# Leaky relu out of PSUM: one parametric relu on ScalarE in place of a multiplication there and a maximum on VectorE

## The chip, the core and the metric

The kernel runs on one core of a Trainium2 chip. The metric is the device time of one execution in microseconds. Before the change three runs gave a median of 1226.71 us (1224.39 to 1227.79). The engines are called as in the profile: PE is TensorE's matmul, PEld its weight load, DVE is VectorE, ACT is ScalarE, POOL is GpSimd, SP is the queue that issues the transfers.

## What is computed

Chunked attention, then two feed-forward layers on its 3072 tokens of 512 features, all in fp32:

```python
scores = scale * np.matmul(q_c, k_full.transpose(0, 1, 3, 2))
...
x = np.ascontiguousarray(attn_out.transpose(0, 2, 1, 3)).reshape(B * S, H * D)
h = x @ w_in                      # 512 -> 2048
g = np.maximum(0.01 * h, h)       # the leaky relu of this change
x = (g @ w_out)                   # 2048 -> 512
return (x @ w_a) * (x @ w_b) @ w_out2
```

## The kernel before

Every fp32 product is made of three matmuls on a high and a low part (`mm3`, L301): a float is cast to fp32r for the high part (an ACT cast), and the difference is the low part (a subtraction on DVE or POOL). So each operand of TensorE costs two passes ahead of it.

The attention works in 24 units of 128 tokens: scores on PE (L202), softmax on DVE and ACT (L215 to L233), turning the probabilities by sixteen 32x32-block transpositions on DVE (`a_turn`, L246; the first four units do it on PE), the product with v on PE (`a_pv`, L276), and hi and lo parts of the result (`a_out`, L289 on ACT, L290 on DVE).

The first feed-forward layer goes over six blocks of 512 tokens (`bi`), and in each over sixteen chunks of 128 hidden features (`f`). `mm1` (L377) makes 12 matmuls into a PSUM tile `h` (two buffers), then the leaky relu: ACT multiplies `h` by 0.01 into `t` (L383), DVE takes the maximum of `t` and `h` into `g` (L385). `split_g` (L317) makes the parts `gh` (ACT, L320) and `gl` (L321, on POOL in the first block, on DVE in the others). `mm2` (L388) adds the chunk's 12 matmuls into four accumulators `a`; it runs two chunks behind `mm1` (`LAG`). In the first block the chunks are halves of 256 tokens that run three chunks apart, so there are 19 steps instead of 16.

Beside the first block the weights are decoded: a raw pair of words is biased on ACT (L79), joined on DVE by three instructions (`w_join`, L83, L86, L87), cast on ACT (L93) and subtracted on POOL (L94) into `w`, which `mm1` and `mm2` of that chunk wait for. There are 32 of these. Beside blocks 1 to 4 the same is done for the second layer's weights (`prep_steps`, tiles `pz`, `ps`, `pw`), whose results go to DRAM. The units of the next block's attention run beside each block.

The second feed-forward layer (`layer3`, `layer4`, L668 on) has products on PE, copies on ACT and sums on DVE; the change does not touch it. Nothing sets the order by hand: the source gives the program's order, and a scheduler that is part of the framework places each engine's instructions from it. Each engine then runs its list in order, and an instruction that waits holds up what stands behind it.

Of the kernel before, what the change touches and what calls it, by code (L numbers as in the profile page):

```python
# [7 lines left out]
F32 = mybir.dt.float32  # L8
F32R = mybir.dt.float32r
I32 = mybir.dt.int32  # L10
AF = mybir.ActivationFunctionType
ALU = mybir.AluOpType
AX = mybir.AxisListType

P = 128
# [11 lines left out]
TB = 512  # L27
# [4 lines left out]
def kernel(  # L32
# [10 lines left out]
    nc = tc.nc  # L43
# [11 lines left out]
    tp = ctx.enter_context(tc.tile_pool(name="tp", bufs=4, side="right"))  # L55
# [251 lines left out]
    def proj(ps, slot, x, c):  # L307
        hi, lo = x
        for kc in range(KC):
            mm3(  # L310
                ps[:, c],
                (slot[:, 0, kc * P:kc * P + P], slot[:, 1, kc * P:kc * P + P]),
                (hi[:, kc, c], lo[:, kc, c]),
                kc == 0, kc == KC - 1,
            )

    def split_g(g, c, eng):  # L317
        gh = tp.tile([P, TB], F32R, tag="gh", name="gh", bufs=3)
        gl = tp.tile([P, TB], F32R, tag="gl", name="gl", bufs=3)
        nc.scalar.copy(gh[:, c], g[:, c])  # L320
        eng.tensor_tensor(  # L321
            out=gl[:, c], in0=g[:, c], in1=gh[:, c].bitcast(F32), op=ALU.subtract
        )
        return gh, gl
# [52 lines left out]
    def mm1(bi, parts):  # L377
        ps = ps_h.tile([P, TB], F32, tag="h", name="h")
        for o, n, f in parts:
            proj(ps, wslot[f, 0], x1["x", bi], slice(o, o + n))  # L380
        c = slice(min(o for o, _, _ in parts), max(o + n for o, n, _ in parts))
        t = tp.tile([P, TB], F32, tag="t", name="t")
        nc.scalar.mul(t[:, c], ps[:, c], 0.01)  # L383
        g = tp.tile([P, TB], F32, tag="t", name="g")
        nc.vector.tensor_tensor(out=g[:, c], in0=t[:, c], in1=ps[:, c], op=ALU.max)  # L385
        return split_g(g, c, nc.gpsimd if bi == 0 else nc.vector)

    def mm2(bi, parts, g):  # L388
# [201 lines left out]
    for n, (bi, f, parts) in enumerate(items):  # L590
# [10 lines left out]
        if first:  # L601
            W1.load(2 * f + 14)
            W1.step(nc.gpsimd)
        behind.append((bi, parts, mm1(bi, parts)))
        if first:
            W1.step(nc.gpsimd)
# [226 lines left out]
```

## Time and profile before

| | |
|---|---|
| median of three runs | 1226.71 us (1224.39 to 1227.79) |
| the profiled execution | 1226.21 us, its span 1224.4 us |
| PE, DVE, ACT, POOL busy | 96%, 61%, 31%, 12% of the span |
| mean granted clock of TensorE | 0.982 |
| first layer (with attention and weights) | about 20 to 590 us |
| second layer | about 590 us to the end |

A row of a group gives its count, the busy time, the mean of one instruction in ns, and the idle time of the engine just before it with what ended that. A row of a timeline gives start and duration in us, and in brackets the idle time before. The clock of a stretch is a share of full speed: 1.00 is 2.4 GHz, 0.5 is 1.2 GHz.

### The profile page before, as it was taken

What the parts mean: (1) busy time and instruction counts of PE and PEld (TensorE: products, weight loads), DVE (VectorE), ACT (ScalarE), POOL (GpSimd) and SP (SyncE); (2) the same over time, 40 slices, a digit from 0 to 9 for tenths busy, and PEclk for the clock granted to TensorE, in tenths of its full rate; (3) what the DMA queues carried; (4) which work ended last, traced back from release to release, by engine and by line L of the source; (5) the groups of instructions that cost most, each with busy time, mean ns of one, the idle gap of its engine ahead of it and who ended that gap; (6) DMA issues with size and microseconds to landing.
All of it is one profiled execution on the core that took longest, in us unless ns stands there. A gap on an engine that the chain in (4) does not pass through costs nothing.

```text
span 1224.4 us, 16825 instructions
## 1 busy us (share of the span) xinstructions
PE 1170.7 (96%) x6632; PEld 984.1 (80%) x6632; DVE 752.9 (61%) x1313; ACT 383.1 (31%) x642; POOL 145.4 (12%) x109
## 2 busy tenths in 40 slices
PE   5788799989998999999999999999999999999998
PEld 5778788867887887888888888888888888888887
DVE  5999959795897899666622443447443447433443
ACT  3634333243334433222422222224122223222220
POOL 1544512032122222000000000000000000000000
PEclk9898999989999999999999999999999999999999
DMA  9766658768887887642633843537453535453512
GB/s 322 256 229 194 210 186 306 268 238 299 297 304 254 310 311 261 212 138 86 221 106 108 319 158 120 193 125 280 162 215 130 198 131 208 158 204 120 189 61 103
DMA packets 63822, 250.72 MB, mean 205 GB/s; under 512 B 7424, under 2 KB 8832, under 8 KB 56832
## 3 DMA queue, kind: packets, MB, share of 16 engines
q1 hardware_dynamic: 63744, 249.66, 57.5%
q8 instruction: 52, 0.85, 0.3%
q14 instruction: 26, 0.21, 0.1%
HBM read 200.34 MB, written 49.28 MB: 204 GB/s over the span
## 4 chain that ended last, share of the span: by engine, by line
PE 67%; DVE 2%; DMA 1%; issue 0%; POOL 0%; SPq 0%; DVEq 0%; POOLq 0%
PE o L729 5%; PE o L730 5%; PE o L731 5%; PE A L662 4%; PE A L663 4%; PE A L664 4%; PE h L303 4%; PE a L403 4%; PE a L404 4%; PE a L400 4%; PE h L304 3%; PE h L305 3%; PE C L662 3%; PE C L663 3%; PE C L664 3%; PE D L663 1%
## 5 line engine op out<-in xcount | busy, mean ns | idle before, releaser
L303 PE MATMUL h<-xh,w 128*128 128x512 f32 (+1 forms) x448 | 168.8, 377 | 17.5 <-POOL w L94 14.7
L400 PE MATMUL a<-gh,w 128*128 128x512 f32 (+1 forms) x448 | 161.3, 360 | 4.8 <-DVE x L412 2.3
L304 PE MATMUL h<-xl,w 128*128 128x512 f32 (+1 forms) x448 | 164.2, 367 | 0.5 <-DVE xl L290 0.5
L305 PE MATMUL h<-xh,w 128*128 128x512 f32 (+1 forms) x448 | 163.7, 365 | 0.0
L403 PE MATMUL a<-gl,w 128*128 128x512 f32 (+1 forms) x448 | 160.8, 359 | 0.0
L404 PE MATMUL a<-gh,w 128*128 128x512 f32 (+1 forms) x448 | 160.8, 359 | 0.0
L303 PEld LDWEIGHTS h<-xh,w 128*128 128x128 f32 x448 | 87.5, 195 | 33.2 <-POOL w L94 15.7
L729 PE MATMUL o<-w,cl 128*128 128x512 f32 x288 | 112.1, 389 | 0.2 <-DMA w<-wod 0.2
L730 PE MATMUL o<-w,ch 128*128 128x512 f32 x288 | 112.0, 389 | 0.0
L731 PE MATMUL o<-w,ch 128*128 128x512 f32 x288 | 112.0, 389 | 0.0
L385 DVE TENSOR_TENSOR g<-t,h 128x512 f32<-128x512 f32 (+1 forms) x99 | 66.1, 668 | 67.3 <-ACT t L383 66.5
L320 ACT CAST gh<-g 128x512 fp32r<-128x512 f32 (+1 forms) x99 | 60.1, 607 | 149.5 <-DVE g L385 144.1
L246 DVE STREAM_TRANSPOSE pt<-p 32x128 f32<-32x128 f32 x320 | 96.8, 302 | 5.5
L400 PEld LDWEIGHTS a<-gh,w 128*128 128x128 f32 x448 | 84.6, 189 | 18.6 <-DVE x L412 2.9
L304 PEld LDWEIGHTS h<-xl,w 128*128 128x128 f32 x448 | 87.7, 196 | 13.1 <-DVE xl L290 0.9
L305 PEld LDWEIGHTS h<-xh,w 128*128 128x128 f32 x448 | 87.0, 194 | 13.3
L404 PEld LDWEIGHTS a<-gh,w 128*128 128x128 f32 x448 | 84.7, 189 | 12.5
L403 PEld LDWEIGHTS a<-gl,w 128*128 128x128 f32 x448 | 84.6, 189 | 12.5
L383 ACT ACTIVATE t<-h 128x512 f32<-128x512 f32 (+1 forms) x99 | 57.5, 581 | 110.3 <-PE h L305 110.3
L684 DVE TENSOR_TENSOR ga<-u,C 128x512 f32<-128x512 f32 x36 | 24.8, 688 | 105.4 <-ACT u L676 76.2
L676 ACT COPY u<-A 128x512 f32<-128x512 f32 x72 | 42.3, 587 | 143.5 <-PE A L664 143.5
L662 PE MATMUL A<-ch,wab 128*128 128x512 f32 x216 | 84.1, 389 | 0.0
(95 smaller groups left out, 2116.3 us busy)
## 6 DMA issues: line engine op xcount, KB each, us to landing
wab<-wab SPq DMA_DIRECT2D x36, 1792.0 KB, 7.3
w<-wod SPq DMA_DIRECT2D x116, 512.0 KB, 4.7
raw<-w SPq DMA_DIRECT2D x68, 512.0 KB, 5.9
wab<-pw SPq DMA_DIRECT2D x12, 1792.0 KB, 6.7
k<-kl SPq DMA_DIRECT2D x48, 256.0 KB, 4.3
v<-vl SPq DMA_DIRECT2D x48, 256.0 KB, 4.7
wod<-w SPq DMA_DIRECT2D x16, 512.0 KB, 5.3
q<-ql SPq DMA_DIRECT2D x48, 128.0 KB, 4.1
```

Of the source, the lines that this page charges most:

```text
L246: nc.vector.transpose(out=pt[o0:o0 + 32, :, 2 * cpar + hpar, hpx, :], in_=p[i0:i0 + 32, hpx::2, 32 * b:32 * b + 32],)
L303: nc.tensor.matmul(ps, w[1], x[0], start=first, stop=False)
L304: nc.tensor.matmul(ps, w[0], x[1], start=False, stop=False)
L305: nc.tensor.matmul(ps, w[0], x[0], start=False, stop=last)
L400: nc.tensor.matmul(ps, slot[:, 1, c], gh[:, t], start=f == 0 and o == 0, stop=False, **kw)
L403: nc.tensor.matmul(ps, slot[:, 0, c], gl[:, t], start=False, stop=False, **kw)
L404: nc.tensor.matmul(ps, slot[:, 0, c], gh[:, t], start=False, stop=f == NF1 - 1, **kw)
L662: nc.tensor.matmul(ps, w[:, 1, i, c], hi[:, kc], start=first and kc == 0, stop=False, **kw)
L663: nc.tensor.matmul(ps, w[:, 0, i, c], lo[:, kc], start=False, stop=False, **kw)
L729: nc.tensor.matmul(o, cl[:, q], w[:, 0, :], start=k == 0, stop=False)
L730: nc.tensor.matmul(o, ch[:, q], w[:, 1, :], start=False, stop=False)
L731: nc.tensor.matmul(o, ch[:, q], w[:, 0, :], start=False, stop=k == NCH - 1)
```

## The change

`mm1` no longer makes `t`. ACT reads `h` from PSUM and writes `g` at once, with a parametric relu whose slope below zero is 0.01.

```diff
         c = slice(min(o for o, _, _ in parts), max(o + n for o, n, _ in parts))
-        t = tp.tile([P, TB], F32, tag="t", name="t")
-        nc.scalar.mul(t[:, c], ps[:, c], 0.01)
         g = tp.tile([P, TB], F32, tag="t", name="g")
-        nc.vector.tensor_tensor(out=g[:, c], in0=t[:, c], in1=ps[:, c], op=ALU.max)
+        nc.scalar.activation(g[:, c], ps[:, c], AF.Prelu, alpha=0.01)
         return split_g(g, c, nc.gpsimd if bi == 0 else nc.vector)
```

99 maxima leave DVE; 99 ACT instructions become another function with the same operands. One tile of the four-buffer tag `t` is taken for each chunk instead of two. Lines behind 383 are two lower in the new kernel. The list of ACT still begins with one load of activation tables and holds no other. The lists of PE are alike but for six small products at the end of the first block, which stand ahead of two matmuls instead of behind them. The lists of DVE and ACT are re-placed by the scheduler at many places; three of them follow.

DVE in the first block, the sixteenfold transposition of the second unit that DVE turns (before; `pt` is the turned probabilities, `z` a joined weight):

```order
L233 TENSOR_TENSOR p<-p,l 128x512
L87 SCALAR_TENSOR_TENSOR z<-raw,z 128x512
L246 STREAM_TRANSPOSE pt_139<-p 32x4x32 x7
L385 TENSOR_TENSOR g<-t,h 128x512
L246 STREAM_TRANSPOSE pt_139<-p 32x4x32 x9
L86 SCALAR_TENSOR_TENSOR z<-raw,z 128x512
```

The same place now:

```order
L233 TENSOR_TENSOR p<-p,l 128x512
L83 TENSOR_SCALAR z<-raw 128x512
L246 STREAM_TRANSPOSE pt_139<-p 32x4x32 x16
L86 SCALAR_TENSOR_TENSOR z<-raw,z 128x512
L87 SCALAR_TENSOR_TENSOR z<-raw,z 128x512
```

The maximum has left the middle of the transpositions, which now stand in one piece.

DVE in the third block (`bi` = 2), the sixteenfold transposition of the last unit turned there (`ps` and `pz` belong to the second layer's weights), before:

```order
L493 TENSOR_TENSOR ps<-pz,ps 128x256
L246 STREAM_TRANSPOSE pt_139<-p 32x4x32 x6
L385 TENSOR_TENSOR g<-t,h 128x512
L246 STREAM_TRANSPOSE pt_139<-p 32x4x32 x4
L321 TENSOR_TENSOR gl<-g,gh 128x512
L246 STREAM_TRANSPOSE pt_139<-p 32x4x32 x6
L83 TENSOR_SCALAR pz<-raw 128x512
```

and now:

```order
L491 TENSOR_TENSOR ps<-pz,ps 128x256
L233 TENSOR_TENSOR p<-p,l 128x512
L246 STREAM_TRANSPOSE pt_139<-p 32x4x32 x16
L321 TENSOR_TENSOR gl<-g,gh 128x512 x2
L83 TENSOR_SCALAR pz<-raw 128x512
```

Here the subtraction `gl` has moved behind the sixteen transpositions too.

ACT in the first block, two chunks (`w<-z` is the cast of a joined weight), before:

```order
L383 ACTIVATE t<-h 128x512
L79 ACTIVATE raw<-raw 128x512
L93 CAST w<-z 128x512
L320 CAST gh<-g 128x512
L79 ACTIVATE raw<-raw 128x512
L93 CAST w<-z 128x512
L79 ACTIVATE raw<-raw 128x512
L383 ACTIVATE t<-h 128x512
```

and now:

```order
L383 ACTIVATE g<-h 128x512
L79 ACTIVATE raw<-raw 128x512
L320 CAST gh<-g 128x512
L79 ACTIVATE raw<-raw 128x512
L93 CAST w<-z 128x512 x2
L79 ACTIVATE raw<-raw 128x512
L93 CAST w<-z 128x512
L383 ACTIVATE g<-h 128x512
```

The cast `gh` stands closer behind the instruction that reads `h`, and what it waits for is now ACT's own work.

## Rows read from the trace of the kernel before

**Rows 1.** The page's busy time of each engine, its share of the span and its instructions.

```profile
PE 1170.7 (96%) x6632; PEld 984.1 (80%) x6632; DVE 752.9 (61%) x1313; ACT 383.1 (31%) x642; POOL 145.4 (12%) x109
```

**Rows 2.** The table of stretches: start and end, length, busy time of PE, PEld, DVE, ACT and POOL (with counts), granted clock, share of the DMA engines, GB/s.

```profile
28.00:152.00 124.00, 99.96 (x918) 95.81 (x919) 118.02 (x186) 57.27 (x101) 62.24 (x45) 0.89 0.68 225
152.00:180.00 28.00, 26.03 (x198) 24.14 (x197) 13.82 (x35) 8.34 (x19) 4.59 (x5) 0.94 0.57 201
...
236.00:274.00 38.00, 32.46 (x205) 26.17 (x204) 36.20 (x77) 14.13 (x25) 10.00 (x6) 0.91 0.69 255
...
320.00:384.00 64.00, 60.51 (x386) 49.88 (x385) 60.09 (x120) 24.22 (x41) 15.84 (x10) 0.97 0.78 279
384.00:590.00 206.00, 204.38 (x1300) 169.37 (x1299) 149.86 (x312) 69.30 (x116) 26.53 (x18) 1.00 0.65 224
590.00:1224.00 634.00, 630.71 (x2779) 520.93 (x2777) 283.91 (x406) 161.79 (x261) 0.00 (x0) 1.00 0.46 167
```

**Rows 3.** Who waited for whom over the whole execution: total us, times, longest.

```profile
ACT gh L320 <- DVE g L385: 144.1, 81, 6.8
...
ACT t L383 <- PE h L305: 110.3, 51, 3.9
...
PE pv L276 <- DVE pt L246: 18.5, 16, 2.7
...
PE h L303 <- POOL w L94: 14.7, 6, 5.8
...
PE a L400 <- DVE x L412: 2.3, 1, 2.3
```

**Rows 4.** The maxima on DVE in the stretch from 28 to 152 us, by shape.

```profile
L385 DVE TENSOR_TENSOR g<-t,h 128x512 f32<-128x512 f32 x12 | 8.1, 678 | 0.1
...
L385 DVE TENSOR_TENSOR g<-t,h 128x256 f32<-128x256 f32 x2 | 0.8, 412 | 0.0
```

**Rows 5.** Shortest, median and longest of the instructions that write or read `g` on DVE.

```profile
L385 DVE TENSOR_TENSOR g<-t,h x99: 402/686/691, 24.8 to 673.7; 128x512 f32<-128x512 f32 x93, 128x256 f32<-128x256 f32 x6
...
L321 DVE TENSOR_TENSOR gl<-g,gh x80: 636/692/1770, 175.6 to 675.1; 128x512 fp32r<-128x512 f32 x80
```

**Rows 6.** The same for the last instruction of a weight's join, whose two inputs are both in SBUF.

```profile
L87 DVE SCALAR_TENSOR_TENSOR z<-raw,z x32: 676/693/1786, 18.6 to 147.5; 128x512 int32<-128x512 int32 x32
```

**Rows 7.** DVE's timeline in the first block: the first and the last of the 14 maxima between 28 and 152 us, and between them two others, each of these with the instruction behind it.

```profile
40.55 0.42 DVE L385 TENSOR_TENSOR g<-t,h 128x256 f32<-128x256 f32 x1
...
57.78 0.68 DVE L385 TENSOR_TENSOR g<-t,h 128x512 f32<-128x512 f32 x1
58.38 1.46 DVE L87 SCALAR_TENSOR_TENSOR z<-raw,z 128x512 int32<-128x512 int32 x1
...
85.37 0.68 DVE L385 TENSOR_TENSOR g<-t,h 128x512 f32<-128x512 f32 x1
85.97 0.68 DVE L86 SCALAR_TENSOR_TENSOR z<-raw,z 128x512 int32<-128x512 int32 x1
...
149.08 0.67 DVE L385 TENSOR_TENSOR g<-t,h 128x512 f32<-128x512 f32 x1
```

**Rows 8.** DVE's timeline in the two later runs without slack: the first and the last of the four maxima of the first run and the `gl` behind the last; then, of the second run, the first and the last of three maxima, and the maximum and the `gl` that stand inside the transpositions from 370.9 to 378.5 us.

```profile
242.08 0.69 DVE L385 TENSOR_TENSOR g<-t,h 128x512 f32<-128x512 f32 x1
...
262.46 0.69 DVE L385 TENSOR_TENSOR g<-t,h 128x512 f32<-128x512 f32 x1
...
264.46 1.75 DVE L321 TENSOR_TENSOR gl<-g,gh 128x512 fp32r<-128x512 f32 x1
...
344.64 0.68 DVE L385 TENSOR_TENSOR g<-t,h 128x512 f32<-128x512 f32 x1
...
367.01 0.68 DVE L385 TENSOR_TENSOR g<-t,h 128x512 f32<-128x512 f32 x1
...
372.81 0.69 DVE L385 TENSOR_TENSOR g<-t,h 128x512 f32<-128x512 f32 x1
...
374.81 1.75 DVE L321 TENSOR_TENSOR gl<-g,gh 128x512 fp32r<-128x512 f32 x1
```

**Rows 9.** PE's timeline behind these two places: what waited, and the first-layer matmuls that follow.

```profile
267.52 0.47 PE L276 MATMUL pv<-pt,v 128*64 128x64 f32 x2 [2.71 <-DVE pt L246]
...
270.50 0.80 PE L303 MATMUL h<-xh,w 128*128 128x512 f32 x1
...
273.61 0.40 PE L304 MATMUL h<-xl,w 128*128 128x512 f32 x1
273.84 0.40 PE L305 MATMUL h<-xh,w 128*128 128x512 f32 x1
...
377.25 0.33 PE L276 MATMUL pv<-pt,v 128*64 128x64 f32 x2 [2.53 <-DVE pt L246]
...
379.57 0.80 PE L303 MATMUL h<-xh,w 128*128 128x512 f32 x1
...
382.73 0.42 PE L304 MATMUL h<-xl,w 128*128 128x512 f32 x1
```

**Rows 10.** ACT's instructions of this size by line: the multiplication that goes, and the exponential of the softmax.

```profile
L383 ACT ACTIVATE t<-h 128x512 f32<-128x512 f32 x93 | 55.2, 594 | 104.9 <-PE h L305 104.9
...
L220 ACT ACTIVATE p<-p 128x512 f32<-128x512 f32 x24 | 15.1, 631 | 47.0 <-DVE p L217 47.0
```

**Rows 11.** The multiplication in the stretch from 28 to 152 us.

```profile
L383 ACT ACTIVATE t<-h 128x512 f32<-128x512 f32 x12 | 7.1, 588 | 0.0
```

## The prediction

> **What bounds the kernel now.** I read the busy shares first. PE is busy 96% of the span, DVE 61%, ACT 31% [rows 1]. The average says that PE is the bound and that an engine at 61% hardly matters; the table of stretches says where that is false. From 590 us to the end PE is busy 630.7 of 634 us, and from 384 to 590 it is busy 204.4 of 206 [rows 2]. No cheaper relu shortens those. PE's gaps lie earlier: 24.0 us between 28 and 152, 2.0 up to 180, 5.5 between 236 and 274 and 3.5 between 320 and 384, each the length less PE's time. One more wait of 2.3 us is for a copy of an accumulator [rows 3]. In three of these stretches DVE is busy 118.0 of 124, 36.2 of 38 and 60.1 of 64 us [rows 2]. So there are places where DVE has no slack, and PE stands idle in just these.
>
> The list of waits tells what PE stands for there: 18.5 us for the product with v behind DVE's transpositions, 14.7 us for first-layer products behind POOL's subtraction of a weight [rows 3]. The second looks like POOL's fault, but POOL is busy only 62.2 of 124 us there: it waits for ACT's cast, which waits for DVE's join. Both waits end at DVE.
>
> The same list has the change's own trail. ACT's cast `gh` stood 144.1 us behind the maximum [rows 3], the largest of the rows shown, and that alone is worth nothing: PE comes to a chunk's `g` two chunks later. What counts is how much earlier the transpositions and the joins end.
>
> **What goes, what comes.** ACT runs 99 instructions before and 99 after. The multiplication on 512 columns takes 594 ns [rows 10]. No parametric relu is in this trace. The nearest rows are that multiplication, with the same tile read from PSUM, and the exponential, a tabulated function on as many columns, 631 ns [rows 10]. I take 594 and hold 631 possible: 99 x 0.037 = 3.7 us over the whole kernel, on an engine that is busy 57 of 124 us even in the fullest stretch [rows 2]. I cost it at nothing; the cover is that ACT idles more than half of the time there. Were the cover gone, the upper end would be those 3.7 us.
>
> DVE loses the 99 maxima. Those that come while DVE has slack are worth nothing. Three stretches remain.
>
> **28 to 152 us.** Here are 12 maxima of 512 columns and 2 of 256 [rows 4]. An instruction that follows without a wait starts 0.60 us after one of 512 columns (57.78 to 58.38, 85.37 to 85.97 [rows 7]); for 256 I take half of the 0.68, 0.34. So 12 x 0.60 + 2 x 0.34 = 7.9 us leave DVE's list.
>
> Not all of it is gained. The two pairs of rows differ behind the maximum: at 85.97 the join runs in 0.68, at 58.38 one takes 1.46 [rows 7]. Over the kernel the maximum's longest is 691 ns with a median of 686 [rows 5], while a join's last step has a median of 693 and a longest of 1786 [rows 6]. So something blocks a join for up to 1.1 us and never a maximum: a maximum in front of a blocked join runs inside the block, and taking it out leaves the join waiting for the same release. I went through the 14 from 40.55 to 149.08 [rows 7] and sorted them by what follows. Four stand in front of a stretched instruction (three of 512 columns, one of 256); one, the last, in front of idle time. The other nine count: eight of 512 and one of 256, 8 x 0.60 + 0.34 = 5.1 us. The Trainium skill, "SBUF — State Buffer", Who interferes with whom, gives a reason: an instruction of VectorE with two SBUF inputs and one of GpSimd lock a shared port pair against each other, and one with at most one SBUF input does not contend. The trace agrees with it (the maximum reads one tile from PSUM and is never stretched). By a count without locks the sum below would be 2.8 us better, by locks that swallow every maximum 5.1 us worse.
>
> I take **5.1 us**, with ends of 0 (all swallowed) and 7.9.
>
> **236 to 274 us.** PE idles 5.5 us, 2.7 of them in one wait for the transpositions [rows 9], in a run of DVE work without slack. Four maxima stand in that run, from 242.08 to 262.46 [rows 8]. Two are followed at once by unstretched work, 1.2 us. The first splits the transpositions of an earlier unit and gives 0.6. The last splits those that PE waits for, and the `gl` at 264.46 behind it is stretched to 1.75 [rows 8]; I count this maximum full, 0.6, because POOL's work that blocks there comes from DVE's own results and moves forward with them. That is 2.4, and I round to 3.0 for the cast `gh` that comes earlier. Ends: 1.2 and 5.5. Behind the wait the clock is low: from 270.50 to 273.61 there are seven gaps between starts, 0.44 each, where 273.61 to 273.84 is 0.23 [rows 9]: the lower level, 1.2 GHz, for 7 x 0.21 = 1.5 us more. The granted clock of the stretch is 0.91 [rows 2]; PE had stood idle before it fell. With most of the wait I take the fall as gone. Together **4.5 us**, ends 1.2 and 7.0.
>
> **320 to 384 us.** PE idles 3.5 us, 2.5 of them before 377.25 [rows 9]. The maximum at 372.81 and a `gl` of 1.75 at 374.81 stand inside the transpositions [rows 8]. In the new list both are gone from there, and the sixteen stand in one piece: 0.6 + 1.75 = 2.4 us, and three more maxima ahead of them with unstretched successors, from 344.64 to 367.01 [rows 8], give 1.8. That is 4.2, over the 3.5 there are, so the wait goes. The clock behind it: the seven gaps from 379.57 to 382.73 take 3.16 us [rows 9], at 0.23 they would take 1.61; 1.5 us. Together **5.0 us**, ends 1.8 and 5.0.
>
> **Elsewhere.** The 2.3 us behind the copy of an accumulator [rows 3] and the 2.0 us from 152 to 180 are not behind a maximum in a way that I can show; nothing, with 4.3 as the upper end. The moved products on PE cost nothing: the same 12 + 12 matmuls. The second layer keeps its list on PE. What is late next where a wait goes is PE itself.
>
> **The sum.** 5.1 + 4.5 + 5.0 = 14.6 us. It is taken off the profiled execution, 1226.2 us, which is 0.5 below the median of 1226.7: **1211.6 us**, 1.2% less. All lower ends (0 + 1.2 + 1.8) give 3.0 us or 1223.2. All upper ends (7.9 + 7.0 + 5.0 + 4.3) give 24.2 or 1202.0; the clock, 0.89 from 28 to 152 [rows 2], could give back some 3 more, an estimate (the low stretches there cost about what the two above did), 1199. About 0.3%, 3.7 us, is what a measurement of this kernel can tell from no change: faster is below 1223.0, slower above 1230.4.
>
> **The rivals.**
>
> *The block takes it all.* The maxima are the work that DVE can do while joins are shut out. With them gone, DVE only waits longer, and POOL, whose `gl` now starts sooner, blocks it at new places. For it: 62 of 124 us are POOL's [rows 2], so a maximum lies beside POOL work half of the time. Against it: nine of 14 maxima have an unstretched successor. Then only the lower ends stand, 1223.2; between this and the forecast 1220. Chance 0.17, half of it within 0.3%.
>
> *More goes.* ACT's casts no longer stand behind a cast that waits for DVE (144.1 us of such waits [rows 3]), so joined weights reach POOL sooner too. Upper ends, 1202; with the clock 1199. Chance 0.13.
>
> *Slower: ACT waits at a worse place.* `gh` stands close behind the relu now, and casts of weights stand behind both. ACT waited for PE before reading `h` 51 times, 110.3 us, 2.2 each [rows 3]. If ACT comes to its relu ahead of PE in the first block, each such wait delays a weight's cast for which PE itself waits later. With 2.2 us on 16 chunks that is 35 us; less the 9.5 us of the two later stretches, 1252. It decides from (9.5 + 3.7) / 16 = 0.8 us for each chunk. Against it: in the stretch from 28 to 152 the multiplication stands at the same kind of place and never had to wait, 0.0 us [rows 11], because DVE's lateness makes ACT late. Chance 0.04.
>
> *The change doesn't do what it says.* If the relu lay in another table than the softmax's exponential, each of the 24 exponentials would cost reloads. The new list of ACT has one load, at its beginning, as before. Then nothing would be lost or won, 1226. Chance 0.03. The Trainium skill, "ScalarE: Activation LUTs", Rules for kernel authors, sends relu and max to VectorE rather than ScalarE, for speed per element. The trace differs for this shape: 594 ns on ACT against 686 on DVE [rows 5, 10], and the ACT pass is there anyway.
>
> **How the numbers follow.** The forecast has 0.63, around 1212 from about 1204 to 1219. Range 1199 to 1222: it takes in "more goes" and most of the swallowed case, and leaves out its end, the slower case and no change, some 0.15. Faster by over 0.3%: 0.63 + 0.13 + half of 0.17 = 0.85. Within: the other half and the case of no effect, 0.11. Slower: 0.04.
>
> **What would show it.** Right: DVE's 99 maxima gone (66 us less busy time), ACT's relu within 594 to 631 ns, the wait of `gh` for DVE gone; PE's gap from 28 to about 147 us near 19; its waits for transpositions near 270 and 370 us almost gone, and the clock at 1.00 there. The second layer takes its 634 us as before. Wrong: as many us of PE's waits as before with stretched joins (the block), PE's waits moved from DVE to ACT (the slower case), or a gap of PE at new transpositions, which would mean that the new order, not the load of DVE, sets them.

## The result, and the profile after

The changed kernel takes **1198.64 us**, the median of 4 runs (1196.63 to 1200.08); the kernel before, on the same chip, 1226.52. The ratio is 0.9773, its 95% interval 0.9751 to 0.9796. The forecast was 1211.6 with a range from 1199 to 1222: the sign was right, the time lies 0.4 us below the range, and the gain of 27.9 us was almost twice the 14.6 of the sum. The profiled execution took 1197.34 us, 28.9 less than that of before.

The busy time of the engines [rows 1] now reads:

```profile
PE 1158.1 (97%) x6632; PEld 975.0 (82%) x6632; DVE 690.7 (58%) x1214; ACT 384.6 (32%) x642; POOL 144.7 (12%) x109
```

DVE has 99 instructions and 62.2 us less, ACT 1.5 us more. PE's 12.6 us less for the same 6632 matmuls fit less time at the low clock (mean granted clock 0.993 against 0.982). The table of stretches answers to [rows 2], in the same columns; the second layer's 634 us now begin at 561:

```profile
28.00:152.00 124.00, 101.71 (x955) 97.17 (x956) 113.13 (x184) 58.94 (x106) 65.75 (x47) 0.93 0.71 237
152.00:180.00 28.00, 28.00 (x221) 25.16 (x220) 13.82 (x29) 9.25 (x20) 4.63 (x5) 1.00 0.64 213
236.00:274.00 38.00, 37.40 (x194) 30.70 (x193) 26.58 (x52) 17.35 (x29) 10.62 (x7) 1.00 0.87 307
320.00:384.00 64.00, 64.00 (x382) 52.85 (x381) 50.29 (x99) 28.69 (x49) 13.46 (x10) 1.00 0.88 313
561.00:1195.00 634.00, 630.89 (x2781) 521.28 (x2779) 273.05 (x390) 161.79 (x261) 0.00 (x0) 1.00 0.46 167
```

Read the PE column first. From 28 to 152 us PE still idles 22.3 us of 24.0. Behind 152 it stands for almost nothing, and the clock there is 1.00 in every row. DVE, which was full in three of these rows, is full in none.

The list of waits, as in [rows 3]:

```profile
ACT g L383 <- PE h L305: 169.7, 62, 4.2
...
PE h L303 <- POOL w L94: 14.5, 8, 5.8
...
PE pv L276 <- DVE pt L246: 7.9, 10, 1.0
```

The wait of `gh` for the maximum (144.1) has no successor. ACT now waits longer for PE, 169.7 us against 110.3: it is ready before its input. PE's wait for transpositions is 7.9 of 18.5, that of `h` for POOL's weights is 14.5 of 14.7 (that of the accumulators' products for them is 2.2, before 0.6), and none is left for a copy of an accumulator. The new instruction costs what the multiplication did [rows 10] (ACT by form: count, busy us, mean ns):

```profile
L320 ACT CAST gh<-g 128x512 fp32r<-128x512 f32 x93 | 57.7, 620 | 2.9
L383 ACT ACTIVATE g<-h 128x512 f32<-128x512 f32 x93 | 55.2, 594 | 159.9 <-PE h L305 159.5
```

**Where the time came from.** PE's list is nearly the same in both kernels, so its progress can be laid side by side: the n-th matmul of line 303 (first pass of the first layer's products; each trace has 448 of them, 128 in block one and 64 in each other block) is the same work in each. In before the 120th starts at 158.1 us, the 128th at 169.8, the 168th at 231.1, the 192nd at 277.5, the 208th at 305.1, the 256th at 386.6, the 336th at 512.6 (counted from 0). The table gives how many us each kernel gained on before within each piece, worked out from such starts in the profiled executions; the first column is from the span's start. A joint is the place where one block ends and the next begins.

| kernel | to 120 | 120–128 | –168 | –192 | –208 | –256 | –336 | sum |
|---|---|---|---|---|---|---|---|---|
| the change | 4.4 | 3.9 | 0.3 | 8.4 | 3.7 | 5.6 | 2.2 | 28.6 |
| e1 load back | 6.7 | 3.9 | 0.3 | 8.6 | 3.7 | 3.5 | −1.9 | 24.9 |
| e2 link back | 1.0 | 0.9 | 0.3 | 7.9 | −0.5 | 5.6 | −5.3 | 9.9 |
| e3 in block one only | 2.6 | 3.9 | −0.7 | 4.7 | 3.3 | 0.5 | −7.4 | 7.0 |
| e4 from block two on | 0.4 | 0.0 | 0.3 | 9.1 | 0.4 | 5.6 | −1.0 | 14.8 |
| e6 last half chunks of block one | 0.4 | 3.7 | −2.8 | 0.9 | −0.2 | −0.5 | 0.3 | 1.8 |
| e8 link back in block one | 2.8 | −1.0 | 0.3 | 8.9 | 2.8 | 5.6 | 2.3 | 21.6 |
| e9 link back from block two on | 3.6 | 3.9 | 0.3 | 7.4 | 0.3 | 5.6 | −4.5 | 16.6 |
| e12 link back in block two | 3.8 | 3.9 | 0.3 | 7.5 | 2.3 | 5.6 | 2.3 | 25.7 |
| e7 units 4 to 7 on PE | 5.5 | 3.0 | 0.4 | 7.8 | −3.0 | 5.6 | 0.9 | 20.2 |
| e5 load back, two SBUF inputs | −2.4 | 3.8 | −0.3 | 4.4 | 2.5 | −1.6 | −3.0 | 3.4 |
| e10 load back in block one | 6.3 | 3.9 | 0.3 | 8.8 | 2.5 | 5.6 | 2.3 | 29.8 |
| e11 before, `gh` on DVE | 0.9 | 0.0 | −3.6 | 3.6 | 3.5 | −0.5 | −2.3 | 1.6 |

The first row says where the sum went wrong: 7.6 us at two joints between blocks (120 to 128 and 192 to 208) that the forecast gave nothing, and 8.4 where it gave 4.5.

### The profile page after: what moved, and what is told of

It reads as the page before. It is cut to its first block, busy times and chain, and to the rows that moved or that the text cites. A ratio compares the mean times of both kernels' runs of the same rounds, so it can differ in the third digit from the quotient of the medians.

```text
span 1195.5 us, 16666 instructions
## 1 busy us (share of the span) xinstructions
PE 1158.1 (97%) x6632; PEld 975.0 (82%) x6632; DVE 690.7 (58%) x1214; ACT 384.6 (32%) x642; POOL 144.7 (12%) x109
## 4 chain that ended last, share of the span: by engine, by line
PE 86%; DVE 9%; DMA 2%; issue 2%; ACT 1%; SPq 0%; DVEq 0%; ACTq 0%
PE h L303 6%; PE a L398 6%; PE a L401 6%; PE a L402 6%; PE h L305 6%; PE h L304 6%; PE o L729 5%; PE o L728 5%; PE o L727 5%; PE A L660 4%; PE A L662 4%; PE A L661 4%; PE C L660 3%; PE C L662 3%; PE C L661 3%; PE s L202 3%
## 5 line engine op out<-in xcount | busy, mean ns | idle before, releaser
L303 PE MATMUL h<-xh,w 128*128 128x512 f32 (+1 forms) x448 | 165.9, 370 | 15.6 <-POOL w L94 14.5
L305 PE MATMUL h<-xh,w 128*128 128x512 f32 (+1 forms) x448 | 161.7, 361 | 0.0
L321 DVE TENSOR_TENSOR gl<-g,gh 128x512 fp32r<-128x512 f32 x80 | 61.8, 772 | 101.6 <-ACT gh L320 101.1
L383 ACT ACTIVATE g<-h 128x512 f32<-128x512 f32 (+1 forms) x99 | 57.5, 581 | 170.0 <-PE h L305 169.7
L303 PEld LDWEIGHTS h<-xh,w 128*128 128x128 f32 x448 | 85.4, 191 | 30.7 <-POOL w L94 17.2
L305 PEld LDWEIGHTS h<-xh,w 128*128 128x128 f32 x448 | 85.4, 191 | 12.9
L660 PE MATMUL A<-ch,wab 128*128 128x512 f32 x216 | 84.1, 389 | 0.2 <-DVE ga L682 0.2
L662 PE MATMUL A<-ch,wab 128*128 128x512 f32 x216 | 84.0, 389 | 0.0
```

The lines of the kernel that those rows point to most:

```text
L303: nc.tensor.matmul(ps, w[1], x[0], start=first, stop=False)
L305: nc.tensor.matmul(ps, w[0], x[0], start=False, stop=last)
L660: nc.tensor.matmul(ps, w[:, 1, i, c], hi[:, kc], start=first and kc == 0, stop=False, **kw)
L662: nc.tensor.matmul(ps, w[:, 0, i, c], hi[:, kc], start=False, stop=kc == HC - 1, **kw)
```

## The experiments

Two theories. **A, the load**: what counts is the 0.6 us of DVE's time that each maximum took; this is the prediction's premise. **B, the link**: ACT runs its list in order, and its cast `gh` stood behind a maximum that stood behind other work in DVE's list; whatever followed `gh` on ACT (a copy of an accumulator, a bias or a cast of a weight) came late too. The change removes both at once, so each is put back alone. Before's own median lay between 1223.83 and 1226.52 us in the sets of runs, so a difference between kernels of different sets is good to some 3 us; the ratios are to before on the same chip. What a kernel's link or load is "worth" is its median less the change's 1198.64.

The scheduler places the lists anew for each kernel, so an edit can also move what it does not name. Compared in the order of their starts, without the relu, the maxima and what the edit adds, DVE's instructions stand in e6 as in before; against the change they differ at some 10 to 20 of 1214 places in e8, e10 and e12, at 60 to 70 in e2 and e9, and at 280 to 300 in e1 and e5 (26 between these two). What e1 says of the load holds a new order of DVE's list as well.

**e1, load back, link gone.** A maximum of the same size whose result nobody reads:

```diff
         nc.scalar.activation(g[:, c], ps[:, c], AF.Prelu, alpha=0.01)
+        j = tp.tile([P, TB], F32, tag="t", name="j")
+        nc.vector.tensor_tensor(out=j[:, c], in0=g[:, c], in1=ps[:, c], op=ALU.max)
```

> The change, and behind each relu a maximum on VectorE of g and h into a tile that nobody reads: VectorE's work of before is back (99 maxima of the same shape, one input from PSUM), but ACT's cast gh no longer waits for it. Theory A (VectorE's time in its runs without slack is what the change gave back, some 19 us of the 28, and only the waits at the block joints, some 8, came from the cast behind the maximum): 1214 to 1222 us. Theory B (the chain relu - VectorE - cast on ACT is what held things up): 1197 to 1204 us.

Measured 1206.44 us (1201.58 to 1207.64; 0.9841 of before, 0.9818 to 0.9864). The load is worth 7.8 us of the 27.9. The profiled execution was its quickest, 1201.58, so the table shows 3.7 of them only: some 6 lost in the last two pieces, 2.3 won in the first.

**e2, link back, load gone.** Eight columns of a maximum (0.16 us) between the relu and `gh`:

```diff
+        d = slice(c.start, c.start + 8)
+        nc.vector.tensor_tensor(out=g[:, d], in0=g[:, d], in1=ps[:, d], op=ALU.max)
```

> The change, and behind each relu a maximum of g and h on 8 columns only, written into g: the cast gh waits for VectorE again as before, but VectorE's work is a small part of before (99 instructions of some 0.1 us). Theory A: 1199 to 1207 us, that is the change's time plus about 1 us a stretch of small instructions and the joints' waits. Theory B: 1215 to 1226 us.

Measured 1215.24 us (1214.08 to 1216.24; 0.9917, 0.9901 to 0.9934): 16.6 us of the gain hang on an operation of 0.16 us. It brings back nearly the whole wait of `gh` (before 144.1):

```profile
ACT gh L320 <- DVE g L385: 132.8, 80, 6.9
```

Measured from before in the same set of runs (1224.94), taking away the load alone (e2) wins 9.7 us, taking away the link alone (e1) 18.5. Both count, and theory A is not the main part. The short maximum also reads `h`, and PE waited 3.4 us in e2 until it had set that tile free (1.1 in the change, for ACT); but e1 and e10, whose unread maximum reads `h` too, have 4.3 us of that wait and are faster, so this is not e2's price. Whether a short maximum ahead of DVE's transpositions would cost as much was not tried.

**e3 and e4, the change in block one only (`if bi == 0`), and in blocks two to six only.**

> The parametric relu in the first block alone, the old pair in the other five. From the two traces the first block's share is 4.4 us up to 152 us and 4.0 at the joint behind it: 1218 us if the shares stand by themselves. If the later stretches gain because the first block let weights and units run ahead: 1205 to 1212. If the first block's lead is given back later: 1222 to 1226.

> The old pair in the first block alone, the parametric relu in the other five. Shares that stand by themselves: 1226.5 less 20.2 = 1206 us. If the later gains hang on the first block: 1214 to 1224.

Measured 1218.2 (1216.92 to 1220.61; 0.9947, 0.993 to 0.9963) and 1210.89 (1210.76 to 1212.68; 0.9888, 0.9874 to 0.9903). By the ratios that is 0.5% and 1.1%, together 1.7 of the change's 2.3%: neither set of blocks is alone the cause, and part of the gain comes only with both: e3 gives back 7.4 us between the 256th and the 336th product.

**The joint of blocks one and two** can be read off the table's second column. It is 3.7 to 3.9 (3.0 in e7) wherever the link is gone from the end of block one, with the load (e1, e5, e10) or without; it is −1.0 to 0.9 wherever it is there (e2, e4, e8, e11). ACT's timeline of before at that place (start, duration, and in brackets the idle time before):

```profile
157.23 0.38 ACT L383 ACTIVATE t<-h 128x256 f32<-128x256 f32 x1
162.12 0.40 ACT L320 CAST gh<-g 128x256 fp32r<-128x256 f32 x1 [4.50 <-DVE g L385]
162.43 0.38 ACT L383 ACTIVATE t<-h 128x256 f32<-128x256 f32 x1
162.70 0.36 ACT L414 COPY x<-a 128x256 f32<-128x256 f32 x1
```

The maximum that `gh` waits for, in DVE's timeline of before:

```profile
156.59 5.04 DVE L246 STREAM_TRANSPOSE pt<-p 32x128 f32<-32x128 f32 x16
161.66 0.42 DVE L385 TENSOR_TENSOR g<-t,h 128x256 f32<-128x256 f32 x1
```

And PE's timeline of before:

```profile
163.12 0.39 PE L400 MATMUL a<-gh,w 128*128 128x256 f32 x1 [1.97 <-ACT x L414]
...
164.86 1.98 PE L276 MATMUL pv<-pt,v 128*64 128x64 f32 x32
```

Read from the bottom. PE needs a PSUM tile that the copy `x` (L414) empties. The copy stands in ACT's list behind `gh`, `gh` waits 4.50 us for a maximum of 0.42, and that stands behind sixteen transpositions of 5.04 us in all. PE waits 1.97 us, and its clock falls: from 160 to 170 us the granted clock is 0.83, and the products with v take 1.98 us where the changed kernel needs 1.15. At the same place in the changed kernel ACT's timeline reads:

```profile
155.31 0.38 ACT L383 ACTIVATE g<-h 128x256 f32<-128x256 f32 x1 [3.44 <-PE h L305]
155.67 0.37 ACT L412 COPY x<-a 128x256 f32<-128x256 f32 x1
155.94 0.41 ACT L320 CAST gh<-g 128x256 fp32r<-128x256 f32 x1
```

The copy follows the relu at once; PE has no wait there in the changed kernel, and the row from 152 to 180 of the table of stretches is full.

**e6, the parametric relu only in the last three half chunks of block one**, all else as before (`if bi == 0 and len(parts) == 1 and parts[0][0]`).

> The kernel before, with the parametric relu only in the last three half chunks of the first block (those whose g is read while the second block begins). Theory B (ACT stands in order behind the cast gh, which waits for the maximum, and a copy of an accumulator or a bias stands behind it): PE's wait of 1.97 us at the copy near 163 us and the low clock behind it go, 4.0 us at the joint of the first and second block, 1222.5; if the weight chain of the second block carries this on to the next joint, 3.7 more, 1218.8. Theory A (only the load of DVE counts): three maxima of 256 columns, 3 x 0.34 = 1.0 us at most, 1225.5 to 1226.5.

Measured 1224.28 us (12 runs, 1220.65 to 1226.17) against 1225.66: 0.9984, 0.9971 to 0.9996. The joint's 3.7 us appear in full where they should, and 2.8 are given back by the 168th product: PE, 3.7 us ahead, meets DVE's still full list and waits 0.49 and 1.25 us at transpositions and 0.48 at a maximum, where in before it had no such wait. A gain at one place lasts only if the engines behind it are ahead as well. The total, 1.4 us less than before, lies between the two forecasts and decides nothing; the joint's 3.7 us do.

**e8, e9 and e12, the link of e2 back in block one alone, in blocks two to six alone, in block two alone** (the two lines of e2 under `if bi == 0`, `if bi > 0`, `if bi == 1`).

> The changed kernel, with a maximum on 8 columns on DVE between the relu and gh in the first block alone: the load stays gone, the wait of gh for DVE is back there. Theory B: what the first block's link costs comes back, 3.4 us up to the 120th first-layer product, 4 at the joint of blocks one and two, and, carried by the chain that prepares the weights, 3.7 at the joint of blocks two and three: 1198.6 + 11 = 1209.7. Rival, no carrying: 1206. Theory A: some 16 + 3 short operations of 0.16 us, of which most hide: 1199 to 1201.

> The changed kernel, with the maximum on 8 columns between the relu and gh in blocks two to six alone. Theory B with carrying: the joints of blocks one to two and two to three keep their gain, since the first block's list is that of the change; what is left of the link's 17 us is 6: 1204.7. Rival (the link costs at its own place in every block): the joint of blocks two and three loses its 3.7 us and later stretches the rest, with the joint of one and two alone kept: 1209. Theory A: 80 operations of 0.16 us beside other work, 1199 to 1202.

> The changed kernel with the maximum on 8 columns between the relu and gh in the second block alone. If a link costs at its own place (the short maximum stands in DVE's list behind sixteen transpositions, ACT's gh waits for it, and the bias of a weight and a copy of an accumulator stand behind gh): the stretch from the 184th to the 208th first-layer product takes some 4 us longer than in the changed kernel, nothing before it changes, 1202.5. If the joint of blocks two and three loses only what lateness the first block hands on: no change, 1198.6.

Measured 1203.93 (1203.02 to 1206.66; 0.9821, 0.9805 to 0.9837), 1210.48 (1209.75 to 1211.19; 0.9871, 0.9856 to 0.9885) and 1201.34 (1200.33 to 1202.95; 0.9824, 0.9806 to 0.9841). Over the change's 1198.64 that is 5.3, 11.8 and 2.7 us; 5.3 and 11.8 make 17.1, e2 had 16.6. So the link is paid in its own block, and the sum is nearly additive. (e12's 2.7 alone is no more than two sets of runs can differ by; the table shows 2.9 for it, 2.3 of them in block two and at its end. e8 came out 2 us under the 1206 that was expected without carrying.) My idea that block one's lateness is carried by the second layer's weights to the next joint is wrong: e8 has that lateness and gains 2.8 from 192 to 208, e9 has none and gains 0.3. What an added 0.16 us does is seen in ACT's timeline of e9 in block two:

```profile
245.77 0.59 ACT L383 ACTIVATE g<-h 128x512 f32<-128x512 f32 x1
252.07 0.62 ACT L320 CAST gh<-g 128x512 fp32r<-128x512 f32 x1 [5.71 <-DVE g L386]
252.59 0.92 ACT L93 CAST pw<-pz 128x512 fp32r<-128x512 f32 x2
253.42 1.04 ACT L93 CAST pw<-ps 128x1024 fp32r<-128x1024 f32 x1
254.37 0.59 ACT L383 ACTIVATE g<-h 128x512 f32<-128x512 f32 x1
259.15 0.62 ACT L320 CAST gh<-g 128x512 fp32r<-128x512 f32 x1 [4.19 <-DVE g L386]
259.67 0.67 ACT L79 ACTIVATE raw<-raw 128x512 f32<-128x512 f32 x1
```

and in DVE's timeline of e9:

```profile
248.67 3.17 DVE L246 STREAM_TRANSPOSE pt<-p 32x128 f32<-32x128 f32 x10
251.87 0.16 DVE L386 TENSOR_TENSOR g<-g,h 128x8 f32<-128x8 f32 x1
```

The same pieces on ACT in the changed kernel:

```profile
244.78 0.60 ACT L383 ACTIVATE g<-h 128x512 f32<-128x512 f32 x1 [0.55 <-PE h L305]
245.41 0.62 ACT L320 CAST gh<-g 128x512 fp32r<-128x512 f32 x1
247.27 0.93 ACT L93 CAST pw<-pz 128x512 fp32r<-128x512 f32 x2 [1.25 <-DMA wab<-pw]
...
252.90 0.66 ACT L79 ACTIVATE raw<-raw 128x512 f32<-128x512 f32 x1 [1.43 <-DMA raw<-w]
```

From `gh` to the bias L79 the changed kernel's list waits only for transfers and for PE, 1.1 to 1.4 us a time; in e9 two waits for DVE of 5.71 and 4.19 us stand in it, and the casts `pw` and the bias are 5.3 and 6.8 us later, of which e9 had lost 0.9 by the 168th product. What PE pays is at the end of that line, in PE's timeline of e9:

```profile
280.56 0.80 PE L401 MATMUL a<-gh,w 128*128 128x512 f32 x1 [2.02 <-DVE x L413]
```

This copy of an accumulator stands in DVE's list behind the first step of a weight's join, which waits for its bias on ACT, in DVE's timeline of e9:

```profile
279.25 0.43 DVE L83 TENSOR_SCALAR pz<-raw 128x512 int32<-128x512 int32 x1 [1.83 <-ACT raw L79]
279.81 0.69 DVE L413 COPY x<-a 128x512 f32<-128x512 f32 x1
```

It is the same wait as the 2.3 us of [rows 3]. The larger part of e9's price, 6.7 us against the change, falls between the 256th and the 336th product: there PE has six short waits for DVE, 3.3 us in all, where the change has none, and its granted clock is 0.50 from 464.8 to 468.2 us. Which step of DVE's list is late there was not followed.

**e7, towards a faster kernel: the change, with units 4 to 7 turned by PE in block one** (`a_turn_pe(u, ps_s, "s")` in place of `a_turn(u)` for `bi == 0`).

> The changed kernel, with the transpositions of units 4 to 7 in the first block made by PE instead of DVE. In the changed kernel PE still idles 22 us from 28 to 152 while DVE is busy 113 of 124. Four units take 4 x 5.1 = 20 us off DVE there and add to PE 64 transpositions and the copies out of PSUM. If DVE's load sets the stretch: some 4 to 8 us less, 1191 to 1195. If the arrival of the first weights by DMA or POOL's subtraction sets it instead, nothing, or PE's added work costs up to 6: 1198 to 1205.

Measured 1206.85 us (1205.35 to 1209.91; 0.9844, 0.9827 to 0.9862), 8.2 slower than the change. DVE is down to 104.05 of 124 us there, and PE reaches the 120th product only 1.1 us sooner. PE's list of waits in e7:

```profile
PE pT L256 <- DVE p L233: 12.3, 4, 4.7
PE h L303 <- POOL w L94: 10.2, 5, 5.8
PE a L398 <- DVE x L410: 6.3, 4, 3.3
```

PE now waits 12.3 us for the softmax itself, which it used to meet one step later. DVE's 9 us less in this stretch did not buy it. Most of the 8.2 us is lost later: at the joint of blocks two and three e7 has −3.0 where the change has 3.7, with two waits of 1.48 and 3.34 us for a copy of an accumulator on DVE.

**e5 and e10: what a load costs in block one.** e5 is e1 with the unread maximum on two SBUF inputs (`in0=g, in1=g`); e10 is e1's maximum in block one only (`if bi == 0`).

> As the run with the whole load put back beside the chain (1206.4), but the unread maximum reads two tiles in SBUF in place of one in PSUM. If two SBUF inputs are what a POOL instruction blocks, the 16 maxima of the first block are now stretched beyond 0.70 us at places, as the joins are, while those with a PSUM input never were. The time: if DVE's time counts in the first block, the stretches of up to 1.1 us on about half of them cost 4 to 8 us more, 1210 to 1214. If it doesn't count there, the time stays within 2 us of 1206.

> The changed kernel with the unread maximum of g and h on DVE in the first block alone. The prediction's 5.1 us for 28 to 152 us were DVE's time there: by it (Theory A) they come back, 1203.7. Theory B: the load of the first block is not what PE waits for, since the whole load in all blocks left PE 6.7 us ahead of the kernel before at the 120th first-layer product, more than the change's 4.4: 1198 to 1200.

e10 measured 1196.19 us (1194.97 to 1197.67; 0.9758, 0.9743 to 0.9774): not slower than the change, whose interval it overlaps, and so the quickest kernel here by nothing that can be told apart. In it DVE is busy 119.35 of 124 us in the first stretch, more than in before:

```profile
28.00:152.00 124.00, 104.75 (x970) 100.78 (x971) 119.35 (x204) 59.48 (x106) 67.27 (x47) 0.92 0.71 238
```

PE works 3 us more there than in the changed kernel. A full DVE is not what holds PE in this stretch. PE's wait for POOL's weights is 10.3 us in e10, against 14.5 in the change.

e5 measured 1219.26 us (9 runs, 1216.3 to 1223.69; 0.9952, 0.9937 to 0.9968), 12.8 over e1, which differs from it in one operand. The unread maximum in e1, from 28 to 152 us (shortest, median and longest in ns):

```profile
L385 DVE TENSOR_TENSOR j<-g,h x15: 407/674/689, 39.4 to 147.3; 128x512 f32<-128x512 f32 x13, 128x256 f32<-128x256 f32 x2
```

and in e5:

```profile
L385 DVE TENSOR_TENSOR j<-g x14: 420/1732/1786, 39.3 to 149.7; 128x512 f32<-128x512 f32 x12, 128x256 f32<-128x256 f32 x2
```

Half of them take 1.73 us or more. One of them in DVE's timeline of e5:

```profile
77.39 1.78 DVE L385 TENSOR_TENSOR j<-g 128x512 f32<-128x512 f32 x1
```

and POOL's timeline of e5 at that time:

```profile
76.88 1.74 POOL L321 TENSOR_TENSOR gl<-g,gh 128x512 fp32r<-128x512 f32 x1
```

The maximum began beside POOL's instruction and ended 0.55 us after it, at 79.17; undisturbed it takes 0.69. PE is 9.1 us behind e1 at the 120th product, more than I had expected of it, and it loses 4.2 and 5.1 us more to e1 from 168 to 192 and from 208 to 256. (The table's e1 is its quickest run and its e5 is one of e5's slower ones, so its sums differ by 21.5 us where the medians differ by 12.8.) So the prediction's block is real and its sorting by inputs right; a load of DVE costs in block one when it is of the blocked kind, and otherwise nothing that shows. The Trainium skill ("SBUF — State Buffer", Who interferes with whom) states just this rule: two SBUF inputs contend with a POOL instruction that reads SBUF, one does not, outside the 2-port modes, which a `tensor_tensor` does not have. The trace agrees: 1732 ns against 674. The prediction left out that exception; a join's first step (L83), with one SBUF input, is stretched too, to 1.52 us at 51.42 in before.

**e11, before with `gh` cast by DVE in blocks two to six**, behind the maximum on the same engine: ACT waits for no maximum, and DVE has more to do.

```diff
-        nc.scalar.copy(gh[:, c], g[:, c])
+        if on_dve:
+            nc.vector.tensor_copy(gh[:, c], g[:, c])
+        else:
+            nc.scalar.copy(gh[:, c], g[:, c])
```

> The kernel before, multiplication and maximum in place, but in blocks two to six the cast gh is DVE's, straight behind the maximum, in place of ACT's. ACT then waits for no maximum there, and DVE has 80 casts of some 0.6 us more. Theory B: the link's share of these blocks (about 12 us by the run with the link in blocks two to six) is won; against it stands 48 us more of DVE's time, at the rate that the whole load cost (7.8 us for 66 us) some 5.7: 1226.5 - 12 + 5.7 = 1220. Theory A (DVE's time): nothing is won and 5.7 or more is lost: 1232 or above.

Measured 1224.0 us (10 runs, 1221.74 to 1226.93) against 1225.28: 0.9989, 0.9976 to 1.0001, no difference. By the load alone it should have been some 6 us slower, by the link's 12 it should have been faster by 6; it is between. The table shows both: 3.5 us gained at the joint from 192 to 208 where e9 has 0.3, 3.6 lost before the 168th product and 2.3 behind the 256th, where DVE's list is fuller. It speaks against A alone, and fits a trade of the link against a load; but theory B's 1220 did not come out either, and DVE's order differs from before's at some 520 places, so it shows no more than that.

## Why the prediction was right in sign and short in size

**The premise failed.** "That alone is worth nothing: PE comes to a chunk's `g` two chunks later." This looked at `gh`'s reader only. What stood behind `gh` on ACT was not asked after. e2 shows its price: 16.6 of 27.9 us. The load of DVE, to which the sum gave all of its 14.6 us, is worth 7.8 (e1) to 9.7 (e2). The rival "more goes" named the first half of this mechanism ("ACT's casts no longer stand behind a cast that waits for DVE") and held 0.13; at 1202, or 1199 with the clock, its time was 0.4 to 3.4 us off. Its second half, that weights reach POOL sooner, does not show in PE's waits for them (14.5 and 2.2 us against 14.7 and 0.6); what came sooner were copies of accumulators and the second layer's casts.

**28 to 152 us: 5.1 forecast, 4.4 seen, for another reason.** The term was DVE's time, "nine of 14 maxima". With all of that time back (e10) PE is 6.3 us ahead, further than with the change; with the link back alone (e2, e8) it is 1.0 and 2.8 ahead. The number agreed by chance, and what was to show it did not come: PE's gap from 28 to 147 us was to be near 19 us, and it is 22.3 (96.71 busy of 119); the idle time fell by 1.7 us, and most of the 4.4 is the clock, 0.93 against 0.89. The kernels with the same source in block one as the change (e3, e9, e12) lie from 2.6 to 3.8, so such a figure is good to some 2 us, and e8's 2.8 does not tell the link from nothing there. "Both waits end at DVE" failed for the second: PE waits for POOL's weights as before, with all maxima gone from DVE. In the sorting of the 14 maxima, three, not four, stand directly in front of a stretched instruction (44.13, 57.78 and 65.05 in DVE's timeline of before), which would have made the term 5.7.

**152 to 180 us and "Elsewhere": 0 forecast.** The 2.0 us there were said to be "not behind a maximum in a way that I can show". They were: PE, copy, `gh`, maximum, sixteen transpositions, four steps that the timelines of three engines show. Worth 3.9 with the clock. The 2.3 us of the other copy [rows 3] went too, 3.7 with the clock (0.83 from 296 to 306 us in before). What decides this second one is not settled: without a link in block two it is gained in e1, e5, e8, e10 and e11 (2.5 to 3.7) and missed in e4 and e7; with one it is missed in e2 and e9 and gained in e3 and e12. A reading that no run tests: the copy is early or late by a step of the weight chain, and several small delays reach that step.

**236 to 274 us: 4.5 forecast, 8.4 seen** (from the 168th to the 192nd product). I let 3.0 of 5.5 us of idle go; 4.9 went (0.6 left). The other 3.5 are for the most part the clock, which was put at 1.5 from the seven gaps behind 270.50. It was low over a longer stretch: the granted clock is 0.50 from 266.7 to 273.5 us, PE is busy 5.16 of these 6.8 us, and half of that, 2.6, would go at the full clock. The products with v from 268.81 on took 1.75 us where the same 26 take 1.03 in the changed kernel. I counted the low stretch from too late a row. Load and link are not told apart here by putting one back: either may return (e1 8.6, e2 7.9) and almost all of the gain stays. With both there e6 has 0.9, but e3, whose first block is the change's, 4.7.

**320 to 384 us: 5.0 forecast, 5.6 seen, for the reason given.** All eight kernels without the load in these blocks have 5.6, with the link (e2, e9) too; those with it have −1.6 to 3.5 (the 3.5 is e1, without the link). This stretch alone is the prediction's: DVE's time, and the clock behind the wait.

**Behind 384 us: 0 forecast, 2.2 seen**, from the 256th to the 336th product. PE's waits of before there (1.11 us for transpositions, 0.51 for `xl`) are gone. Both causes bear on it: with the link alone e2 and e9 are 5.3 and 4.5 worse than before, with the load alone e1 1.9. But e4, which has neither in these blocks, is 1.0 worse than before, so the piece also hangs on what the earlier blocks hand on.

**Costs.** The relu at 594 ns on 512 columns was right. The slower rival (ACT waits for `h` at a worse place) did come as a wait, 169.7 us against 110.3, and little cost of it shows: PE's waits for POOL's weights are 1.4 us longer in all (14.5 and 2.2 against 14.7 and 0.6).

## What to carry to other kernels

A wait in an in-order list is priced by what stands behind it in that list, not by who reads its result. Before calling a cross-engine wait harmless, walk down the waiting engine's timeline to the next few instructions and ask of each who needs it; where an operation can be folded into its neighbour on the same engine, the round trip that goes may be worth more than the operation. And a gain at one place is kept only as far as the other engines come forward too (e6), so parts measured apart need not add up.

## What the runs showed of the hardware

- A maximum of 512 columns on DVE took 674 ns (median, 28 to 152 us) with one input in PSUM and 1732 with both in SBUF, beside the same POOL work; the kernel with the second kind was 12.8 us slower.
- More work on DVE in block one (16 chunks' maxima, e10) did not slow the kernel: 1196.19 against 1198.64 us. Why PE is then 2 us further at the 120th product was not tried.
- Short waits of PE carry a second price: in before the granted clock was 0.83 from 160 to 170 and from 296 to 306 us, around and behind waits of 1.97 and 2.25 us; the pieces that hold them became 3.9 and 3.7 us shorter when the waits went. Not every such wait has it: in e2 PE waited 2.59 us at the first of these places, and the granted clock from 160 to 170 us was 1.00.
